# Attention, a gated layer and a normalised layer on one core: the splits move from GpSimd to ScalarE and VectorE, and TensorE gets more filler matmuls around the first scores

## The chip, the core and the metric

One core of a Trainium2 chip runs the whole program. The metric is the device time of one execution in microseconds (us); "before" is the median of three runs. The profile is of one more execution of the same program, recorded by the hardware profiler. Its engines are TensorE (PE, with PEld for its weight loads), VectorE (DVE), ScalarE (ACT), GpSimd (POOL) and SyncE (SP, which issues the DMAs).

## The reference, cut to what matters

```python
scores = scale * np.matmul(q, k.transpose(0, 1, 3, 2))     # q, k, v: 2 x 12 heads x 448 x 64
scores = np.where(mask, -1e9, scores)                       # causal
attn = softmax(scores); attn_out = np.matmul(attn, v)
x = attn_out as (896 tokens, 768)
gate = 1.0 / (1.0 + np.exp(-(x @ w_gate)))                  # w_gate, w_val: 768 x 1536
val = x @ w_val
x = gate * val @ w_out                                      # w_out: 1536 x 768
h = x @ w_in                                                # 768 x 1024
solu = h * softmax(h)
ln = (solu - mean) / np.sqrt(var + 1e-06) * g_ln
out = ln @ w_out2                                           # 1024 x 768
```

## The kernel before, in words

Every product that has to be close to float32 is made of three matmuls in a reduced format (fp32r): a value is split into a **high part** (a copy that rounds) and a **low part** (the value minus the high part), and high x high, high x low and low x high are summed in PSUM. So each tensor that TensorE reads costs two elementwise instructions on some other engine, and the change is about which engine makes them.

**Attention.** Two heads make a pair; there are 12 pairs. A loop of numbered slots, four to a head (96 of them, and some to drain), issues the work of all engines by hand: in slot s the scores of s (`sc_mm`, L350, two slots at a time), the row maximum (`sc_max`, DVE L359), the exponential of slot s-2 (`sc_exp`, ACT L365), and, a few slots later, transposes of the probabilities (`tr_mm`, L416, into one of two PSUM buffers), their split (`tr_hi` on ACT L423, `tr_lo` on DVE L231), the transposes of the reciprocal sums (`rs_mm`, tile r, L388) and the product with v (`pv_mm`, L445). Scores go into one of four PSUM buffers, and a buffer comes free when the exponential has read it. The splits of q, k, v are "side steps": the table `SIDE` gives the slot of each within its pair, `ENG` its engine (A ScalarE, D VectorE, P GpSimd). The names that matter: kh0, kh1 are the high parts of k of the pair's first and second head, kl0, kl1 the low parts, qh and ql those of q. A head's q and k arrive in one buffer (tile qkr) of a ring of four; the load of head h+4 is issued on SP when head h has been split. Each engine takes its instructions in the order in which they were issued, so a step that waits holds up all that stands behind it.

Before the loop, TensorE multiplies an identity matrix 30 times into a PSUM tile that nobody reads (tile warm, L315), and the splits of heads 0 and 1 are issued.

**Gated layer** (L600): 24 chunks of weights, two (gate, value) to each of 12 tiles t; a chunk is a stationary block hl[high, low] of 128 x 768. Weights come from DRAM as 64-bit words (tile raw, two buffers) and are turned into float32 by one ScalarE and three VectorE instructions (`bits_steps`, L112 to L120, tile t). `start_chunk(c)` and `mid_chunk(c)` are called at the beginning and in the middle of the matmuls of chunk c; they prepare chunk c+1 and c+2. A "rider" is a tile of the third layer's weights (wi), prepared in the same way at the middle of certain chunks. After the value chunk the gate is applied (`gate_val`): sigmoid on ACT (L183), product on DVE (L186), high part on ACT (L188), low part on POOL (L189).

**Output projection** (L627, 12 more chunks), **third layer** (L657) and **last product** (L718) follow; `w_hi`, the high part of every weight chunk, is on POOL (L131), `w_lo` on DVE (L135).

Of the kernel before, what the change touches and what calls it, by code (L numbers as in the profile page):

```python
# [44 lines left out]
def attn_moe_moe2(ctx: ExitStack, tc: tile.TileContext, qk, v, w_gv, w_out, w_in2, w_out2, g_ln, out):  # L45
# [87 lines left out]
    def w_lo(it, hi, lo, g=None):
        if g is None:
            nc.vector.tensor_tensor(out=lo, in0=t_t.pop(it), in1=f32(hi), op=ALU.subtract)  # L135
        else:
            nc.vector.scalar_tensor_tensor(out=lo, in0=t_t.pop(it), scalar=g, in1=f32(hi),
                                           op0=ALU.mult, op1=ALU.subtract)
# [54 lines left out]
    with ExitStack() as actx:  # L193
# [122 lines left out]
        for h in range(2):
            prep_k_hi(h)
            prep_q_hi(h)
            if h == 0:
                prep_k_lo(h, 'D', False)  # L320
# [465 lines left out]
```

## Time and profile before

| | |
|---|---|
| three runs | 518.37, 518.78, 519.37 us; median 518.78 |
| profiled execution | 518.95 us, span from the first to the last instruction 517.2 us |
| granted TensorE clock, mean | 0.993 of full speed |
| PE / DVE / ACT / POOL busy | 97% / 70% / 39% / 43% of the span |

The span is what the views below cover; 518.95 - 517.2 = 1.75 us of the execution lie around it. Busy shares are means over stages that differ: in attention all engines are nearly full, after it TensorE alone is.

### The profile page before, as it was taken

The page shows a single profiled execution, that of the slowest core. Times are in us where ns is not written, and L with a number is a line of the kernel's source. Part 1 is how long each engine was busy: PE and PEld are TensorE (multiplying, and loading weights), DVE is VectorE, ACT ScalarE, POOL GpSimd, SP SyncE. Part 2 cuts the span into 40 slices and gives each one's busy share as a digit, 9 for nine tenths or more (in the row PEclk, how much of TensorE's full clock was granted, in tenths as well). Part 3 has the DMA queues.
Part 4 walks back from the last instruction along what each step waited for, and adds up shares of the span by engine and source line. Part 5 has one row for each costly group of instructions (what it writes and reads, how often), then busy time and mean ns, then how long its engine had stood idle before and what let it go on. Part 6 is the DMA issues. An engine that isn't in the chain of part 4 may idle for free. (4 is left out here: it accounts for less than half of the span.)

```text
span 517.2 us, 7582 instructions
## 1 busy us (share of the span) xinstructions
PE 502.7 (97%) x2786; PEld 455.7 (88%) x2786; DVE 360.9 (70%) x542; ACT 200.3 (39%) x446; POOL 220.0 (43%) x299
## 2 busy tenths in 40 slices
PE   5999999989999999999999999999999999999997
PEld 5899898878999988888889899999998888899997
DVE  5998999987565887887787775777872888741210
ACT  5888887874223223232313221221122433332211
POOL 4999999972333133333223330111151577820000
PEclk8899999999999999999999999999999999999999
DMA  7955454112323434334434332344431231000101
GB/s 206 289 156 148 113 150 126 43 61 73 130 104 103 160 125 159 106 107 157 163 125 160 122 116 82 128 163 163 128 123 54 69 116 63 0 32 30 62 32 61
DMA packets 15125, 58.30 MB, mean 113 GB/s; under 512 B 2160, under 2 KB 2672, under 8 KB 15088
## 3 DMA queue, kind: packets, MB, share of 16 engines
q1 hardware_dynamic: 15088, 57.81, 34.9%
q8 instruction: 22, 0.36, 0.3%
q14 instruction: 15, 0.12, 0.1%
HBM read 55.05 MB, written 2.75 MB: 112 GB/s over the span
## 5 line engine op out<-in xcount | busy, mean ns | idle before, releaser
L600 PE MATMUL gv<-xy,hl 128*128 128x448 f32 x828 | 170.5, 367 | 3.0 <-DVE hl L135 3.0
L600 PEld LDWEIGHTS gv<-xy,hl 128*128 128x128 f32 x828 | 154.6, 188 | 18.8 <-DVE hl L135 5.8
L627 PE MATMUL pm<-g,hl 128*128 128x448 f32 x432 | 89.4, 368 | 0.0
L627 PEld LDWEIGHTS pm<-g,hl 128*128 128x128 f32 x432 | 81.1, 188 | 8.2
L112 ACT ACTIVATE raw<-raw 128x768 f32<-128x768 f32 (+1 forms) x56 | 47.4, 857 | 55.0 <-DMA raw<-in_wo_dram 26.7
L115 DVE TENSOR_SCALAR t<-raw 128x768 int32<-128x768 int32 (+1 forms) x56 | 40.9, 730 | 34.3 <-ACT raw L112 33.0
L117 DVE SCALAR_TENSOR_TENSOR t<-raw,t 128x768 int32<-128x768 int32 (+1 forms) x56 | 59.4, 1061 | 1.9
L718 PE MATMUL po<-wo,lt 128*128 128x384 f32 x336 | 60.5, 339 | 0.0
L189 POOL TENSOR_TENSOR g<-wk,g 128x448 fp32r<-128x448 f32 x24 | 27.3, 1158 | 77.8 <-ACT g L188 77.8
L657 PE MATMUL h<-wi,xy 128*128 128x512 f32 x252 | 59.2, 395 | 0.0
L718 PEld LDWEIGHTS po<-wo,lt 128*128 128x128 f32 x336 | 58.7, 188 | 0.1
L657 PEld LDWEIGHTS h<-wi,xy 128*128 128x128 f32 x252 | 47.2, 187 | 11.4
L120 DVE SCALAR_TENSOR_TENSOR t<-raw,t 128x768 int32<-128x768 int32 (+1 forms) x56 | 54.9, 980 | 1.7
L131 POOL TENSOR_SCALAR hl<-t 128x768 fp32r<-128x768 f32 x36 | 34.0, 943 | 42.6 <-PE pm L627 31.6
L365 ACT ACTIVATE p<-s,sum 128x448 f32<-128x448 f32 (+1 forms) x96 | 45.5, 480 | 16.0 <-DVE sum L359 16.0
L445 PE MATMUL x<-pt,v 128*128 128x448 f32 (+3 forms) x252 | 48.7, 327 | 0.0
L350 PE MATMUL s<-qks 128*128 128x448 f32 (+1 forms) x192 | 42.8, 321 | 4.0 <-ACT p L365 2.5
L445 PEld LDWEIGHTS x<-pt,v 128*128 128x128 f32 x252 | 37.1, 190 | 2.0 <-ACT rb L221 1.3
L350 PEld LDWEIGHTS s<-qks 128*128 128x128 f32 x192 | 32.4, 199 | 6.9 <-POOL qks L231 3.2
L359 DVE TENSOR_REDUCE sum<-s 128x1 f32<-128x448 f32 (+1 forms) x96 | 36.3, 409 | 0.9 <-PE s L350 0.9
L135 DVE TENSOR_TENSOR hl<-t,hl 128x768 fp32r<-128x768 f32 x36 | 34.3, 952 | 3.7 <-POOL hl L131 3.6
L131 POOL TENSOR_SCALAR wi<-t 128x512 fp32r<-128x512 f32 x12 | 7.4, 618 | 66.3 <-DVE t L120 66.3
(90 smaller groups left out, 583.6 us busy)
## 6 DMA issues: line engine op xcount, KB each, us to landing
raw<-in_gv_dram SPq DMA_DIRECT2D x24, 768.0 KB, 4.3
raw<-in_wo_dram SPq DMA_DIRECT2D x20, 768.0 KB, 4.3
qkr<-in_qk_dram SPq DMA_DIRECT2D x46, 224.0 KB, 4.0
raw<-in_wi_dram SPq DMA_DIRECT2D x12, 512.0 KB, 3.5
vr<-in_v_dram SPq DMA_DIRECT2D x12, 256.0 KB, 2.8
out_dram<-o SPq DMA_DIRECT2D x6, 384.0 KB, 2.3
qkr<-in_qk_dram SPq DMA_DIRECT2D x4, 112.0 KB, 2.6
out_dram<-o SPq DMA_DIRECT2D x2, 192.0 KB, 1.9
```

The costliest lines, as they stand in the source:

```text
L112: nc.scalar.activation(out=w1.bitcast(F32), in_=w1.bitcast(F32), func=AF.Copy, scale=2.0 ** -112)
L115: nc.vector.tensor_scalar(out=tt, in0=w1, scalar1=3, scalar2=None, op0=ALU.logical_shift_left)
L117: nc.vector.scalar_tensor_tensor(out=tt, in0=w1, scalar=-2 ** 31, in1=tt, op0=ALU.bitwise_and, op1=ALU.bitwise_or)
L120: nc.vector.scalar_tensor_tensor(out=tt, in0=w0, scalar=29, in1=tt, op0=ALU.logical_shift_right, op1=ALU.bitwise_or)
L131: nc.gpsimd.tensor_scalar(out=hi, in0=t_t[it], scalar1=g, scalar2=1.0, op0=ALU.mult, op1=ALU.mult)
L350: nc.tensor.matmul(out=o, lhsT=l, rhs=r, start=(m == 0), stop=(m == 2))
L365: nc.scalar.activation(out=p_t[h % NPB][:, POFF[i]:POFF[i] + n], in_=ps_sc.pop(s), func=AF.Exp, bias=mx, scale=1.0, accum_out=sm)
L445: nc.tensor.matmul(out=ps[:, 128 * j:], lhsT=l, rhs=pt_t[h][:, c, u, c0:c0 + S - 128 * j], start=(n == 0), stop=(n == 20))
L600: nc.tensor.matmul(out=ps[i, b], lhsT=w[:, a, cs], rhs=xy[kk][:, x, b * S:(b + 1) * S], start=(kk == 0 and a == 0 and x == 0), stop=(kk == ...
L627: nc.tensor.matmul(out=ps[b], lhsT=w[:, a, cs], rhs=g_t[kk][:, x, b * S:(b + 1) * S], start=(kk == 0 and a == 0 and x == 0), stop=(kk == N ...
L657: nc.tensor.matmul(out=h[:, n * 512:(n + 1) * 512], lhsT=xy[kk][:, a, tk], rhs=wi[n * NK + kk][:, c], start=(kk == 0 and i == 0), stop=(kk ...
L718: nc.tensor.matmul(out=ps[n], lhsT=lts[k // 4][:, a, k % 4], rhs=wo[k][:, c, cs], start=(k == 0 and i == 0), stop=(k == NF2 - 1 and i == 2))
```

## The change

1. `w_hi` (the high parts of the chunks and the riders) goes from GpSimd to ScalarE. In the last stage the two uses of it keep GpSimd.
2. The gate's low part goes from GpSimd to VectorE, and is issued one step later, behind the products of both batches.
3. `chunk_lo(c + 1)` moves from the middle of chunk c to its start, ahead of the bit steps of chunk c+2; riders move from chunks 6, 8, ..., 20 to 7, 9, ..., 21.
4. In attention kh0 goes from VectorE to ScalarE, kl0 from GpSimd to VectorE, and ql0, ql1, kl0 change slots.
5. Around the start: 56 filler matmuls in place of 30, and 24, 8 and 8 more behind the scores of slots 2, 4 and 6; q's high part of head 0 on VectorE; the low parts of head 1 are issued inside the loop, behind the maxima of slots 0 and 1; small moves among the memsets.

```diff
-    rider = {6 + 2 * n: n for n in range(8)}
+    rider = {7 + 2 * n: n for n in range(8)}
...
-    def w_hi(it, hi, g=1.0):
-        nc.gpsimd.tensor_scalar(out=hi, in0=t_t[it], scalar1=g, scalar2=1.0, op0=ALU.mult, op1=ALU.mult)
...
+    def w_hi(it, hi):
+        nc.scalar.copy(out=hi, in_=t_t[it])
...
     def start_chunk(c):
         chunk_hi(c + 1)
+        chunk_lo(c + 1)
...
     def mid_chunk(c):
-        chunk_lo(c + 1)
...
         nc.scalar.copy(out=g[:, 0], in_=gf)
-        nc.gpsimd.tensor_tensor(out=g[:, 1], in0=gf, in1=f32(g[:, 0]), op=ALU.subtract)
+        yield
+        nc.vector.tensor_tensor(out=g[:, 1], in0=gf, in1=f32(g[:, 0]), op=ALU.subtract)
         yield
...
-        ENG = dict(rx='P', qh0='P', qh1='P', kh0='D', kh1='A', kl0='P', kl1='P', vh='P', vl='P', xh='A', xl='P', rr='A', lk='P')
+        ENG = dict(rx='P', qh0='P', qh1='P', kh0='A', kh1='A', kl0='D', kl1='P', vh='P', vl='P', xh='A', xl='P', rr='A', lk='P')
...
-        for _ in range(30):
-            nc.tensor.matmul(out=ps[:, :128], lhsT=identb, rhs=identb, start=True, stop=True)
...
+        keep_warm(56)
+        prep_k_hi(0)
+        prep_k_lo(0, 'D', False)
+        prep_q_hi(0, 'D')
+        prep_q_lo(0)
+        prep_k_hi(1)
+        prep_q_hi(1)
+        load_qk(4)
...
         SIDE = dict(
-            rm=12, rx=10, ql1=-2, rc=10, xh=22, qh0=-7, kh0=-6, xm=21, ql0=-4, sm=9, kl0=-1, qh1=-4, kh1=-3, kl1=-1,
+            rm=12, rx=10, ql1=-1, rc=10, xh=22, qh0=-7, kh0=-6, xm=21, ql0=-5, sm=9, kl0=-3, qh1=-4, kh1=-3, kl1=-1,
...
             at(sc_mm, s)
+            if s in (2, 4, 6):
+                keep_warm(24 if s == 2 else 8)
...
             at(sc_max, s)
+            if s == 0:
+                prep_k_lo(1, 'D', False)
+            if s == 1:
+                prep_q_lo(1)
+                load_qk(5)
...
                         ev[b].send(ps[1, b])
+                for b in bs:
+                    if i:
+                        next(ev[b])
...
-            w_hi(("o", k), wo[k][:, 0])
+            nc.gpsimd.tensor_scalar(out=wo[k][:, 0], in0=t, scalar1=1.0, scalar2=1.0, op0=ALU.mult, op1=ALU.mult)
```

**VectorE before the first scores and just after.** The line numbers of the two versions differ by a few: L231 and L228 are the low parts of k (64x448) and of the transposes (pt), L252 and L249 the low part of q, L359 and L355 a row maximum (tile sum). Before:

```order
L231 TENSOR_TENSOR qks<-qkr,qks 64x448
L252 SCALAR_TENSOR_TENSOR qks<-qkr,qks 128x448 x2
L359 TENSOR_REDUCE sum_148<-s 128x1 x2
L225 CAST qks<-qkr 128x448
L359 TENSOR_REDUCE sum_148<-s 128x1 x2
```

and in the change:

```order
L228 TENSOR_TENSOR qks<-qkr,qks 64x448
L242 TENSOR_SCALAR qks<-qkr 128x448
L249 SCALAR_TENSOR_TENSOR qks<-qkr,qks 128x448
L355 TENSOR_REDUCE sum_148<-s 128x1
L228 TENSOR_TENSOR qks<-qkr,qks 64x448
L355 TENSOR_REDUCE sum_148<-s 128x1
L249 SCALAR_TENSOR_TENSOR qks<-qkr,qks 128x448
L355 TENSOR_REDUCE sum_148<-s 128x1
```

The first maximum no longer stands behind q's low part of head 1 (the second of the "x2"), and k's low part of head 1 (the second 64x448) is now VectorE's.

**VectorE over the second half of a pair in attention.** L225 is kh0, L452 and L448 scale a finished pair by the reciprocal sums (xf). Before:

```order
L225 CAST qks<-qkr 128x448
L231 TENSOR_TENSOR pt<-t,pt 128x512
L359 TENSOR_REDUCE sum_150<-s 128x1 x2
L252 SCALAR_TENSOR_TENSOR qks<-qkr,qks 128x448
L231 TENSOR_TENSOR pt<-t,pt 128x512
L359 TENSOR_REDUCE sum_150<-s 128x1
L452 TENSOR_TENSOR xf<-x,rb 128x448
L359 TENSOR_REDUCE sum_150<-s 128x1
L252 SCALAR_TENSOR_TENSOR qks<-qkr,qks 128x448
L231 TENSOR_TENSOR pt<-t,pt 128x512
L359 TENSOR_REDUCE sum_150<-s 128x1 x2
```

and in the change:

```order
L228 TENSOR_TENSOR pt<-t,pt 128x512
L355 TENSOR_REDUCE sum_150<-s 128x1
L249 SCALAR_TENSOR_TENSOR qks<-qkr,qks 128x448
L355 TENSOR_REDUCE sum_150<-s 128x1
L228 TENSOR_TENSOR pt<-t,pt 128x512
L355 TENSOR_REDUCE sum_150<-s 128x1
L448 TENSOR_TENSOR xf<-x,rb 128x448
L228 TENSOR_TENSOR qks<-qkr,qks 64x448
L355 TENSOR_REDUCE sum_150<-s 128x1
L228 TENSOR_TENSOR pt<-t,pt 128x512
L355 TENSOR_REDUCE sum_150<-s 128x1
L249 SCALAR_TENSOR_TENSOR qks<-qkr,qks 128x448
```

The cast kh0 is gone, kl0 (64x448) has come in, and each q low part, which stood right ahead of a transposes' low part (pt), now stands between two maxima.

**VectorE in the gated layer, from one value chunk to the next.** L115, L117 and L120 are the three bit steps (768 wide a chunk, 512 wide a rider), L135 and L134 the low parts of a chunk (hl) or a rider (wi), L186 and L182 the gate's product (wk). Before:

```order
L135 TENSOR_TENSOR wi_2519<-t,wi_2519 128x512
L115 TENSOR_SCALAR t<-raw 128x768
L117 SCALAR_TENSOR_TENSOR t<-raw,t 128x768
L120 SCALAR_TENSOR_TENSOR t<-raw,t 128x768
L135 TENSOR_TENSOR hl<-t,hl 128x768
L186 TENSOR_TENSOR wk<-gv,wk 128x448 x2
L115 TENSOR_SCALAR t<-raw 128x768
```

and in the change, where L186 is the gate's low part (g):

```order
L134 TENSOR_TENSOR hl<-t,hl 128x768
L115 TENSOR_SCALAR t<-raw 128x768
L117 SCALAR_TENSOR_TENSOR t<-raw,t 128x768
L120 SCALAR_TENSOR_TENSOR t<-raw,t 128x768
L115 TENSOR_SCALAR t<-raw 128x512
L117 SCALAR_TENSOR_TENSOR t<-raw,t 128x512
L120 SCALAR_TENSOR_TENSOR t<-raw,t 128x512
L182 TENSOR_TENSOR wk<-gv,wk 128x448 x2
L186 TENSOR_TENSOR g_2483<-wk,g_2483 128x448 x2
L134 TENSOR_TENSOR hl<-t,hl 128x768
L134 TENSOR_TENSOR wi_2518<-t,wi_2518 128x512
```

The low part of the next chunk has moved from behind the chunk's three bit steps to ahead of them, and the gate's two low parts have come in behind its products.

**ScalarE over the same stretch.** L112 is its part of the bit steps, L183 and L179 the sigmoid, L188 and L184 the gate's high part. Before:

```order
L112 ACTIVATE raw<-raw 128x768
L112 ACTIVATE raw<-raw 128x512
L183 ACTIVATE wk<-gv 128x448 x2
L112 ACTIVATE raw<-raw 128x768
L188 CAST g_2427<-wk 128x448 x2
```

and in the change, where L131 is `w_hi`:

```order
L131 CAST hl<-t 128x768
L112 ACTIVATE raw<-raw 128x768
L179 ACTIVATE wk<-gv 128x448 x2
L131 CAST hl<-t 128x768
L112 ACTIVATE raw<-raw 128x768
L112 ACTIVATE raw<-raw 128x512
L131 CAST wi_2518<-t 128x512
L184 CAST g_2483<-wk 128x448 x2
```

Each chunk's high part now stands ahead of ScalarE's share of the bit steps, and the rider's high part stands ahead of the gate's.

## Rows read from the trace of the kernel before

**Rows 1.** The page: busy time of each engine; the chain that ended last.

```profile
PE 502.7 (97%) x2786; PEld 455.7 (88%) x2786; DVE 360.9 (70%) x542; ACT 200.3 (39%) x446; POOL 220.0 (43%) x299
...
PE 44%; ACT 0%; issue 0%
```

**Rows 2.** Waits: engine, line, waited for; us in total, times, longest us.

```profile
PEld gv L600 <- DVE hl L135: 5.8, 8, 0.9
...
PEld r L388 <- POOL rx L223: 2.9, 9, 1.2
...
PEld t L416 <- PE s L350: 1.7, 8, 0.2
```

**Rows 3.** Windows around the first scores: busy us (instructions) of each engine, granted clock.

```profile
7.90:10.40 2.50, 0.03 (x1) 0.00 (x0) 2.00 (x5) 1.21 (x5) 2.33 (x3) 0.68 1.03 227
10.40:15.70 5.30, 5.16 (x23) 4.42 (x24) 3.67 (x9) 4.25 (x16) 3.99 (x6) 0.50 1.05 270
```

**Rows 4.** Timeline of the start: start us, duration us, instruction, [idle before].

```profile
1.61 3.38 PE L315 MATMUL warm<-identb 128*128 128x128 bf16 x30 [1.61 <-DVE identb L289]
...
4.74 0.62 DVE L231 TENSOR_TENSOR qks<-qkr,qks 64x448 fp32r<-64x448 f32 x1 [1.07 <-ACT qks L221]
...
6.69 0.82 PE L350 MATMUL s<-qks 128*128 128x448 f32 x4
...
7.71 0.56 ACT L221 CAST qks<-qkr 128x448 fp32r<-128x448 f32 x1 [3.00 <-DMA qkr<-in_qk_dram]
...
8.37 0.63 DVE L252 SCALAR_TENSOR_TENSOR qks<-qkr,qks 128x448 fp32r<-128x448 f32 x1 [1.74 <-POOL qks L242]
...
8.91 0.75 DVE L359 TENSOR_REDUCE sum<-s 128x1 f32<-128x448 f32 x2
...
9.69 0.55 DVE L225 CAST qks<-qkr 128x448 fp32r<-128x448 f32 x1
...
10.44 0.77 PE L350 MATMUL s<-qks 128*128 128x448 f32 x2 [2.51 <-ACT p L365]
```

**Rows 5.** Timeline of TensorE: the first transpose of r in three pairs.

```profile
26.61 0.30 PE L388 MATMUL r<-identx,rx 128*128 128x128 f32 x1
...
35.09 0.33 PE L388 MATMUL r<-identx,rx 128*128 128x128 f32 x1
...
97.32 0.33 PE L388 MATMUL r<-identx,rx 128*128 128x128 f32 x1
```

**Rows 6.** Window over seven pairs of attention, columns as in rows 3.

```profile
35.09:97.32 62.23, 61.79 (x478) 55.93 (x477) 57.48 (x120) 50.64 (x161) 59.99 (x85) 1.00 0.46 119
```

**Rows 7.** Groups in that window, by form: xcount | busy us, mean ns | idle before.

```profile
L231 POOL TENSOR_TENSOR qks<-qkr,qks 64x448 fp32r<-64x448 f32 x14 | 18.5, 1341 | 0.0
...
L252 DVE SCALAR_TENSOR_TENSOR qks<-qkr,qks 128x448 fp32r<-128x448 f32 x14 | 14.4, 1029 | 0.0
...
L225 DVE CAST qks<-qkr 128x448 fp32r<-128x448 f32 x7 | 4.8, 680 | 0.0
```

**Rows 8.** Windows after attention: tile t=2; t=6; t=4 to 11; second output tile.

```profile
149.00:163.58 14.58, 14.58 (x73) 13.52 (x72) 9.17 (x10) 3.67 (x6) 4.20 (x4) 1.00 0.30 103
208.22:223.48 15.26, 14.86 (x74) 13.39 (x72) 12.17 (x15) 4.47 (x7) 4.81 (x5) 1.00 0.42 139
...
178.18:300.47 122.29, 119.27 (x577) 107.23 (x576) 95.43 (x110) 34.89 (x55) 37.89 (x39) 1.00 0.41 139
...
315.35:330.23 14.88, 14.88 (x73) 13.52 (x72) 11.06 (x14) 3.36 (x5) 2.25 (x3) 1.00 0.31 109
```

**Rows 9.** Timeline at the start of tile t=6.

```profile
208.59 0.95 DVE L135 TENSOR_TENSOR hl<-t,hl 128x768 fp32r<-128x768 f32 x1
...
209.59 1.48 PE L600 MATMUL gv<-xy,hl 128*128 128x448 f32 x6 [0.40 <-DVE hl L135]
```

**Rows 10.** Groups from 194.33 to 300.47 us, by form, columns as in rows 7.

```profile
L189 POOL TENSOR_TENSOR g<-wk,g 128x448 fp32r<-128x448 f32 x14 | 15.9, 1159 | 40.6 <-ACT g L188 40.6
...
L112 ACT ACTIVATE raw<-raw 128x768 f32<-128x768 f32 x14 | 12.7, 905 | 20.0 <-DMA raw<-in_gv_dram 20.0
```

More of the change, by code (lines that the diff above doesn't have):

```diff
@@ L128, in bits, with w_lo @@
             pass
-    def w_hi(it, hi, g=1.0):
-        nc.gpsimd.tensor_scalar(out=hi, in0=t_t[it], scalar1=g, scalar2=1.0, op0=ALU.mult, op1=ALU.mult)
[L133 to L138, printed above, removed]
+    def w_hi(it, hi):
+        nc.scalar.copy(out=hi, in_=t_t[it])
+    def w_lo(it, hi, lo):
+        nc.vector.tensor_tensor(out=lo, in0=t_t.pop(it), in1=f32(hi), op=ALU.subtract)
     def chunk_hi(c):
@@ L244, in prep_q_hi @@
             else:
-                nc.scalar.activation(out=t[:, 1], in_=qk_raw[h][:, 0], func=AF.Copy, scale=0.125)
+                nc.vector.tensor_scalar(out=t[:, 1], in0=qk_raw[h][:, 0], scalar1=0.125, scalar2=None, op0=ALU.mult)
         def prep_k_hi(h, eng='A'):
@@ L253, in prep_q_lo, with prep_k_lo @@
                                            op0=ALU.mult, op1=ALU.subtract)
-        def prep_k_lo(h, eng='P', last=True):
+        def prep_k_lo(h, eng='P', load=True):
             t = qk_sp[h]
             sub(eng, t[D:, 0], qk_raw[h][D:, 1], f32(t[D:, 0]))
-            if last:
-                qk_raw.pop(h)
+            if load:
                 load_qk(h + 4)
@@ L285, in attn_moe_moe2 @@
         make_identity(nc, ident)
-        nc.gpsimd.tensor_copy(out=identx[:, :D], in_=ident[:, D:])
-        nc.gpsimd.tensor_copy(out=identx[:, D:], in_=ident[:, :D])
         nc.vector.tensor_copy(out=identb, in_=ident)
@@ L291, in attn_moe_moe2 @@
         nc.gpsimd.memset(mask0, 0.0)
+        nc.gpsimd.tensor_copy(out=identx[:, :D], in_=ident[:, D:])
+        nc.gpsimd.tensor_copy(out=identx[:, D:], in_=ident[:, :D])
         nc.gpsimd.affine_select(out=mask0, in_=mask0, pattern=[[-1, 128]], compare_op=ALU.is_ge,
@@ L307, in attn_moe_moe2 @@
                 nc.vector.memset(p_t[i][:, POFF[j] + QE[j]:POFF[j + 1]], 0.0)
-            nc.vector.memset(p_t[i][:, POFF[3] + QE[3]:], 0.0)
         for i in range(2):
@@ L311, in attn_moe_moe2, with keep_warm @@
                 nc.scalar.copy(out=v2[i][:, a, :, D:2 * D], in_=zero.rearrange("p (j d) -> p j d", j=3))
+            nc.vector.memset(p_t[i][:, POFF[3] + QE[3]:], 0.0)
         ps = ps_x.tile([128, S], F32, tag="x", name="warm")
-        for _ in range(30):
-            nc.tensor.matmul(out=ps[:, :128], lhsT=identb, rhs=identb, start=True, stop=True)
[L316 to L320, printed above, removed]
-                prep_q_lo(h)
-            else:
-                prep_q_lo(h)
-                prep_k_lo(h, 'P', False)
-            qk_raw.pop(h)
-            load_qk(h + 4)
+        def keep_warm(n):
+            for _ in range(n):
+                nc.tensor.matmul(out=ps[:, :128], lhsT=identb, rhs=identb, start=True, stop=True)
+        keep_warm(56)
[6 more added lines that the diff above has]
+        load_qk(4)
         rs_t, rx_t, rb_t, pt_t, ps_sc, ps_tr, ps_pv, ps_rr, xf_t = {}, {}, {}, {}, {}, {}, {}, {}, {}
@@ L565, in attn_moe_moe2 @@
             ev.send(pre[t, 1])
+            next(ev)
     gpb = gctx.enter_context(tc.tile_pool(name="gpb", bufs=1, reuse_waits="tile"))
```

## The prediction, made before the changed kernel ran

> **What bounds the kernel now.** I read the page first: TensorE is busy 97% of the span, the next engine 70%, and the chain that ended last is TensorE alone [rows 1]. So only time in which TensorE stands still, or runs at half its clock, can be won, and the other engines matter only where they make it wait. Then the list of waits [rows 2] and windows by stage. Three places come out.
>
> *The start.* TensorE idles from 7.9 to 10.4 us, the granted clock falls to 0.50 meanwhile (1.2 GHz in place of 2.4; the mean of that stretch is 0.68), and the next 5.3 us of matmuls run at 0.50 [rows 3].
>
> *Attention.* The first transposes of r are a pair's mark: 26.61 to 35.09 is 8.48 us, 35.09 to 97.32 is 7 pairs of 8.89 [rows 5]. TensorE's work is the same in each, so every later pair loses about 0.41 us. The waits name two places, each once per pair: r waits for rx, GpSimd's last step in a row of them, and a transposes' group t waits some 0.2 us [rows 2]. The "PE s" named there cannot be it, as TensorE always runs behind its own scores; what the group needs is one of two PSUM buffers, freed by VectorE's tr_lo. GpSimd is busy 59.99 of 62.23 us, VectorE 57.48, ScalarE 50.64 [rows 6].
>
> *The gated layer.* A tile's 72 matmuls take 14.58 us undisturbed (t=2) and 15.26 in t=6 [rows 8]. The fifth matmul of t=6, the first that reads a low part, starts at 209.59, when VectorE's hl has ended (208.59 + 0.95) [rows 9]; eight such waits are listed [rows 2]. From t=4 to 11 the stage takes 122.29 us where 8 x 14.58 = 116.64 would do: 5.65 us lost.
>
> **The change, part by part.**
>
> *Gated layer.* The late hl stands behind three bit steps of another chunk, and these wait for a load: ScalarE's share of them stood idle 20.0 us for the DMA in 14 chunks [rows 10]. With the low part ahead of the bit steps, it needs only its high part, whose chunk landed one chunk earlier. I walk one tile from TensorE's first matmul, 0. VectorE makes two products (0.62 each, 209.46 on, just behind that hl), ScalarE two high parts of the gate behind them (0.56 each, as the cast at 7.71 [rows 4]), to about 2.1. The chunk's high part on ScalarE is not in the trace; nearest is its 768-wide L112, 905 ns [rows 10] (bounds 0.56, a 448-wide cast, and 0.96, that scaled to 768): to 3.0. Low part 0.95 [rows 9]: ready at 4.0, wanted at 7.3 (half a tile). Slack 3.3 us. The value chunk: sigmoids to 8.6, high part 9.5, low part 10.4, wanted at 14.6: slack 4.2. The gate's low part on VectorE is new: GpSimd takes 1159 ns [rows 10]; the nearest VectorE rows of two SBUF operands and 448 columns are 0.62 us when GpSimd is quiet (at 4.74 and 8.37 [rows 4]) and 1029 when not [rows 7]. GpSimd has nothing left to do here, so 0.62; 1.24 a tile. VectorE's work becomes 12.17 + 1.24 = 13.4 of 14.58 [rows 8], less what GpSimd's absence shortens. It fits. What is queued behind the new waits: ScalarE's high part of the rider waits for VectorE's bit steps at about 14.8, and the gate's high parts stand behind it; they are not wanted before VectorE's products at 15 anyway. Of the 5.65 us I take back 4.9: the listed waits, 5.8 [rows 2], include in each the little that lies between any two loads, and the rest of the loss is a slightly wider spacing of some matmuls (below), which I leave. Bounds 0 and -5.7.
>
> *Attention.* kl0 takes 1341 ns on GpSimd [rows 7], a share of 15% of a pair; without it rx can come up to 1.3 us earlier, and r no longer waits. On VectorE it costs 0.62 (at 4.74 [rows 4]); kh0 goes, 0.68 [rows 7], and costs ScalarE 0.56 (at 7.71 [rows 4]). VectorE's sum hardly changes: 57.48 + 7 x (0.62 - 0.68) = 57.1 over seven pairs, which at 8.48 have 59.4 us: 96%. But the order does: a q low part of 1029 ns stood right ahead of tr_lo; now a maximum, or 0.62 of kl0, does. 1029 is the price beside GpSimd's 1341; alone it is 0.63 (at 8.37 [rows 4]), so VectorE falls below 96%. ScalarE: 50.64 + 7 x 0.56 = 54.6, 92%. I take 0.36 of 0.41 us in seven pairs, -2.5. Bounds: 0, and -2.9.
>
> *Start.* The first maximum no longer waits for head 1 (8.91 before, [rows 4]; about 7.6 now, when the scores that begin at 6.69 are done). k's low part of head 1 on VectorE follows its high part (7.71 + 0.56) and is ready at 8.9. But slot 5 needs the PSUM buffer of slot 1, and ScalarE's exponential of slot 1 now stands behind kh of head 2, whose load lands near 9.6 (the cast at 9.69 [rows 4]). So the scores of slot 4 and 5 start near 10.5 again, not earlier. The gain is the clock: 5.16 us of matmuls at 0.50 [rows 3] take about half at full clock, 2.6 less. The fillers: 30 took 3.38 us [rows 4], 0.107 from start to start when the last one's length is taken off, and 128 columns at 1.2 GHz are 0.107 us: the low level. At 6.69 the level was the high one, four score matmuls in 0.82 us against two in 0.77 at 10.44 [rows 4]. So the clock rose between 4.9 and 6.7. If in the middle, near 5.5, some 36 of the 56 are done by then and 20 more at half the price end at 6.6: the scores start on time. If late, 56 x 0.107 end at 7.6 and the scores are 0.9 late. The 24 lie in what was idle. The two groups of 8 are paid: 16 x 0.055 = 0.9. Waits for exponentials, and scores that start a little late, take some 0.4 back. I take -1.3; bounds -2.6, when the fillers hide in waits, and +1.7, when the clock falls all the same and the 16 cost 0.107.
>
> What the row shows is one execution with 0.50 from about 9 to 15.7 us [rows 3], and one place of the rise. The Trainium skill ("TensorE: Matmul & The Clock Gate", section "What's actually happening") says that the gate does not start its count with the kernel, so that the place where the clock rises shifts from run to run. By the row the sum below stands at 510.2; by the page the start can come out at the worse bound in some runs, which is the second rival's time. No single trace can show which.
>
> *Edits at nothing.* The memsets lie in the wait for the first load. The rider's shift by one chunk moves work off VectorE's even chunk. Loads of head 4 and 5 follow the same splits as before; the order of chunk loads changes by one place. In the output projection TensorE did not wait (14.88, x72, busy all through [rows 8]); ScalarE has 3.36 of 14.88 there and takes on 2 x 0.9.
>
> **Sum.** 518.95 (the profiled execution: span 517.2 and 1.75 around it) - 4.9 - 2.5 - 1.3 = 510.25; the median of the runs is 0.17 lower. Predicted: 510.2.
>
> **Rivals.**
>
> 1. *Attention keeps 8.89 us a pair*, because ScalarE takes the wait over: kh0 now stands between two exponentials, and one of them frees the PSUM buffer of the next scores. For: ScalarE goes to 92%. Against: it has 59.4 - 54.6 = 4.8 us left in seven pairs, 0.7 in each, and takes on 0.56 once a pair, not ahead of every score. Time: 510.2 + 2.5 = 512.7.
> 2. *The clock falls at the start as before*, since TensorE still idles some 0.5 to 1 us between the fillers and the scores of slot 4, or since the 56 begin at a bad moment. The second is what the skill's page would have. For: 2.5 us of idling were enough before [rows 3]. Against: less than half of that is left. The start then gives +0.5 in place of -1.3: 512.0.
> 3. *ScalarE in the gated layer*: chunk high parts, waiting behind the gate's, come too late, and half of the stalls return. For: ScalarE takes its instructions in order, and the gate's wait for TensorE. Against: over 3 us of slack. 510.2 + 2.45 = 512.7.
> 4. *VectorE becomes the bound of the gated layer; slower than before.* In t=6 it works 12.17 of 15.26 us and waits 3.1 [rows 8]. If all its waits stay, 1.24 more makes a tile 16.5: 8 tiles x (16.5 - 14.58) = 15.4 in place of 5.65, +9.7 - 2.5 - 1.3 on 518.95: 524.7 after the 0.17. It decides where waits exceed 14.58 - 13.41 = 1.2 us a tile. Against: GpSimd, whose work beside VectorE's stretched it (0.63 against 1.03 [rows 4, 7]), is out of this stage, so the 12.17 shrinks.
>
> One thing more shifts the sum without being a rival: 72 matmuls take 14.58 us in the gated layer but 14.88 in the output projection [rows 8], same shape, no wait. If a stage takes on the other's spacing, that is 6 x 0.30 = 1.8 less or 11 x 0.30 = 3.3 more.
>
> **How the numbers follow.** Forecast 0.60; rival 1 0.15; rival 2 0.08; rival 3 0.07; rival 4 0.05; nothing moves, or gains cancel, 0.05. What a measurement can tell from no change is about 0.2%, 1 us. Forecast and rivals 1 to 3 are faster: 0.90, less 0.02 for two of them together with the wider spacing: 0.88 faster, 0.06 same, 0.06 slower. The range: below, the spacing's 1.8 and the attention's and start's other bounds, 507.0; above, rivals 1 to 3 and two of them at once, 515.0.
>
> **What will show it.** Right: pairs of 8.5 us between r's; no wait of TensorE for hl and tiles of 14.6; granted clock 1.00 from about 5 us on; GpSimd idle in the gated layer. Wrong: a wait of the scores for ScalarE's p (rival 1), 0.50 between 9 and 16 us (2), hl waiting for ScalarE (3), VectorE over 95% in a tile of over 15 us (4). What would make me wrong most is a wait whose place in the order I walked with a duration taken from a quieter stretch.

## The result, and the profile after

The changed kernel takes 513.98 us (median of 4 runs, 513.41 to 514.42) against 518.58 (4 runs, 517.47 to 519.37) of the kernel before: a ratio of 0.9912, 95% interval 0.9891 to 0.9933. It is 4.6 us faster where 8.4 were forecast; the time lies in the range given. Most kernels here, the one before too, have some executions 2 to 5 us longer than the rest, with a wider spacing of the matmuls (last section), so I compare stages of profiled executions and say where their spacing differs. The profiled execution took 514.42 us, 2.45 of it outside the span.

The page of the changed kernel; the busy times, then the chain that ended last by line:

```profile
PE 501.6 (98%) x2852; PEld 459.5 (90%) x2852; DVE 350.8 (69%) x567; ACT 239.5 (47%) x505; POOL 136.2 (27%) x214
...
PE gv L604 33%; PE pm L634 17%; PE po L725 12%; PE h L664 11%; DVE sum L355 3%; DVE qks L249 3%; DVE pt L228 2%; PE s L346 2%; PE t L412 1%; DVE xf L448 1%; PE x L441 1%; DVE qks L228 1%; PE tp L707 1%; PE r L384 1%; ACT p L361 1%
```

Three lines of VectorE stand in the chain, sum (L355), qks (L249) and pt (L228): in attention the end now goes through VectorE. The waits that answer to [rows 2]:

```profile
PEld s L346 <- ACT p L361: 9.1, 22, 0.9
...
PEld r L384 <- POOL rx L220: 1.9, 2, 1.1
...
PE s L346 <- ACT p L361: 1.6, 4, 0.6
```

The wait of gv for hl is gone, that of a transposes' group t too, and that of r for rx comes twice, not nine times. In their place the scores wait for ScalarE's exponentials, 22 times. Windows that answer to [rows 3, 6, 8]: the start, seven pairs of attention, the tile t=6:

```profile
7.90:10.40 2.50, 2.00 (x29) 1.67 (x27) 2.28 (x6) 1.83 (x7) 1.00 (x2) 1.00 1.02 234
10.40:15.70 5.30, 4.87 (x47) 4.26 (x48) 5.13 (x11) 4.63 (x16) 2.17 (x3) 1.00 1.07 275
...
35.87:99.40 63.53, 62.18 (x478) 56.48 (x477) 59.57 (x120) 54.19 (x169) 51.98 (x78) 1.00 0.44 117
...
208.41:223.00 14.59, 14.59 (x74) 13.52 (x73) 11.33 (x17) 6.48 (x10) 0.00 (x0) 1.00 0.43 144
```

The granted clock is 1.00 all through the start. Seven pairs take 63.53 us, 9.08 each, where they took 62.23. A gated tile takes 14.59, and GpSimd does nothing in it. By stage, from first instruction to first instruction:

| stage | before | after | difference | forecast |
|---|---|---|---|---|
| up to the first transpose of r | 18.55 | 18.65 | +0.10 | -1.3 |
| from there to the twelfth pair's | 96.25 | 98.15 | +1.90 | -2.5 |
| from there to the gated layer | 12.30 | 12.26 | -0.04 | 0 |
| gated layer | 173.37 | 167.81 | -5.56 | -4.9 |
| output projection | 89.28 | 87.55 | -1.73 | 0 |

With +0.13 behind these the span is 5.20 us shorter; 0.67 came back outside it. So the gated layer gave what was forecast, the projection took the narrower spacing that was named as open, and attention went the wrong way. No run shows that the edits chose that spacing; without its 1.73 us the profiled spans differ by 3.5.

Where the 9.08 come from, in the timeline of one pair:

```profile
57.95 1.14 POOL L228 TENSOR_TENSOR xy<-xf,xy 128x448 fp32r<-128x448 f32 x1
...
58.16 1.42 DVE L249 SCALAR_TENSOR_TENSOR qks<-qkr,qks 128x448 fp32r<-128x448 f32 x1
...
59.50 0.34 DVE L355 TENSOR_REDUCE sum<-s 128x1 f32<-128x192 f32 x1
...
59.94 0.42 ACT L361 ACTIVATE p<-s,sum 128x192 f32<-128x192 f32 x1 [0.98 <-DVE sum L355]
...
60.50 0.19 PEld L346 LDWEIGHTS s<-qks 128*128 128x128 f32 x1 [0.38 <-ACT p L361]
...
61.63 0.56 ACT L218 CAST qks<-qkr 128x448 fp32r<-128x448 f32 x1
...
62.02 0.67 DVE L249 SCALAR_TENSOR_TENSOR qks<-qkr,qks 128x448 fp32r<-128x448 f32 x1
...
62.08 0.32 ACT L361 ACTIVATE p<-s,sum 128x64 f32<-128x64 f32 x1
...
62.19 1.38 POOL L228 TENSOR_TENSOR v<-vr,v 128x384 fp32r<-128x384 f32 x1
...
62.54 0.19 PEld L346 LDWEIGHTS s<-qks 128*128 128x128 f32 x1 [0.35 <-ACT p L361]
```

Two waits a pair. (a) ql1, one slot later now, runs at 58.16 for 1.42 us; the maximum behind it starts at 59.50, the exponential at 59.94 after 0.98 us of idling, and TensorE's scores stand 0.38 us for the PSUM buffer which that exponential frees. ql1 is long as well as late: a GpSimd difference began 0.21 us ahead of it, at 57.95, while ql0, which begins at 62.02 ahead of GpSimd's 62.19, takes 0.67. (b) kh0, the CAST at 61.63, holds ScalarE for 0.56 us; the exponential behind it starts at 62.08, and the scores stand 0.35 us.

### The profile page after: what moved, and what is told of

The parts are those of the page before. It is cut to its first block, busy times and chain, and to the rows that moved or that the text cites. A ratio compares the mean times of both kernels' runs of the same rounds, so it can differ in the third digit from the quotient of the medians.

```text
span 512.0 us, 7710 instructions
## 1 busy us (share of the span) xinstructions
PE 501.6 (98%) x2852; PEld 459.5 (90%) x2852; DVE 350.8 (69%) x567; ACT 239.5 (47%) x505; POOL 136.2 (27%) x214
## 4 chain that ended last, share of the span: by engine, by line
PE 81%; DVE 12%; ACT 2%; issue 2%; POOL 1%; DMA 1%; SPq 1%; DVEq 0%; POOLq 0%; ACTq 0%
PE gv L604 33%; PE pm L634 17%; PE po L725 12%; PE h L664 11%; DVE sum L355 3%; DVE qks L249 3%; DVE pt L228 2%; PE s L346 2%; PE t L412 1%; DVE xf L448 1%; PE x L441 1%; DVE qks L228 1%; PE tp L707 1%; PE r L384 1%; ACT p L361 1%
## 5 line engine op out<-in xcount | busy, mean ns | idle before, releaser
L604 PE MATMUL gv<-xy,hl 128*128 128x448 f32 x828 | 168.0, 365 | 0.0
L634 PE MATMUL pm<-g,hl 128*128 128x448 f32 x432 | 87.7, 365 | 0.0
L651 POOL TENSOR_SCALAR t<-t,g_sb 128x768 f32<-128x768 f32 x8 | 9.0, 1128 | 248.7 <-PE pm L634 248.7
L134 DVE TENSOR_TENSOR hl<-t,hl 128x768 fp32r<-128x768 f32 x36 | 34.5, 958 | 41.0 <-ACT hl L131 39.3
L117 DVE SCALAR_TENSOR_TENSOR t<-raw,t 128x768 int32<-128x768 int32 (+1 forms) x56 | 53.4, 954 | 1.9
L112 ACT ACTIVATE raw<-raw 128x768 f32<-128x768 f32 (+1 forms) x56 | 47.9, 865 | 10.5 <-DMA raw<-in_wo_dram 6.1
L120 DVE SCALAR_TENSOR_TENSOR t<-raw,t 128x768 int32<-128x768 int32 (+1 forms) x56 | 51.2, 913 | 1.7
L346 PE MATMUL s<-qks 128*128 128x448 f32 (+1 forms) x192 | 46.4, 321 | 3.3 <-ACT p L361 1.6
L355 DVE TENSOR_REDUCE sum<-s 128x1 f32<-128x448 f32 (+1 forms) x96 | 38.6, 413 | 1.6 <-PE s L346 1.1
L171 DVE TENSOR_TENSOR lt<-tp,lt 128x512 fp32r<-128x512 f32 x14 | 9.7, 691 | 36.4 <-ACT lt L170 36.4
L115 DVE TENSOR_SCALAR t<-raw 128x768 int32<-128x768 int32 (+1 forms) x56 | 31.1, 555 | 4.4 <-ACT raw L112 4.4
L131 ACT CAST hl<-t 128x768 fp32r<-128x768 f32 x36 | 30.0, 833 | 7.3 <-PE pm L634 4.2
```

What stands on the lines that cost most here:

```text
L112: nc.scalar.activation(out=w1.bitcast(F32), in_=w1.bitcast(F32), func=AF.Copy, scale=2.0 ** -112)
L117: nc.vector.scalar_tensor_tensor(out=tt, in0=w1, scalar=-2 ** 31, in1=tt, op0=ALU.bitwise_and, op1=ALU.bitwise_or)
L120: nc.vector.scalar_tensor_tensor(out=tt, in0=w0, scalar=29, in1=tt, op0=ALU.logical_shift_right, op1=ALU.bitwise_or)
L346: nc.tensor.matmul(out=o, lhsT=l, rhs=r, start=(m == 0), stop=(m == 2))
L355: nc.vector.reduce_max(out=sums_of(s)[1], in_=ps_sc[s], axis=AX.X, negate=True)
L604: nc.tensor.matmul(out=ps[i, b], lhsT=w[:, a, cs], rhs=xy[kk][:, x, b * S:(b + 1) * S], start=(kk == 0 and a == 0 and x == 0), stop=(kk == ...
```

## The experiments

My theory after this trace: the gated layer holds all the gain; attention loses by waits (a) and (b), each made by one instruction's place; the start's gain is handed to waits for ScalarE and GpSimd. The rivals stand in each expectation. "Pair" is the distance between the first transposes of r of two pairs, as a mean of the seven from the third to the tenth where nothing else is said. Each ratio is to the kernel before as timed beside it (median 518.93 us in experiments 1 to 4, 518.04 in 5 to 8, 517.47 in 9 to 12), so ratios, and stages of traces, are what to compare. Edits are cut to the parts of lines that change.

**1. The gated layer's edits alone.** The kernel before with the diff's first part (rider, w_hi, chunk_lo, gate_val); ENG, SIDE and the start as before.

> The kernel before with the gated layer's edits alone (high parts on ScalarE, gate's low part on VectorE, the chunk's low part moved forward, riders shifted). Theory: all that was won comes from here, 5.6 us in the gated layer and 1.7 in the output projection, and the rest of the change costs some 2: tiles of 14.59 us in both stages, r transposes of attention still 8.89 us apart, 511.3 us. Rival: the two stages need the changed attention's order too (its chunks 0 and 1 are prepared there); then waits for hl stay at some tiles, and the time is 513 to 516.

512.63 us, ratio 0.9906 (0.9872 to 0.9940); pairs 8.89; tiles and output tiles 14.59. There is no wait for hl, and the gated layer takes 167.81 us as in the changed kernel. So these edits alone give the whole gain, with the narrow spacing in the projection; attention keeps its old length. The rival is out; the median is 1.3 us above the theory's.

**2. kh0 back on VectorE.**

```
-kh0='A', kh1='A', kl0='D'
+kh0='D', kh1='A', kl0='D'
```

> The changed kernel with kh0 back on VectorE. Theory (two new waits in each pair, each from one moved step): the wait of the scores of slot 5 for the exponential behind kh0, about 0.23 us, goes; the wait of slot 3's scores behind ql1 stays; pairs of about 8.85 us, 514.0 - 10 x 0.23 = 511.7 us. Rival (the pair is bound by what VectorE has to do in all): VectorE gets 0.68 us more a pair, pairs of 9.3 us or more, 516 us or more.

521.29 us, ratio 1.0089 (1.0052 to 1.0125): slower than before; pairs 9.76. My expectation was wrong, the rival right. The window and the group in attention, one kl0 with the GpSimd step beside it in the timeline, and last the same two steps in the changed kernel:

```profile
36.00:97.00 61.00, 55.28 (x433) 51.08 (x432) 60.44 (x112) 47.79 (x146) 46.67 (x71) 1.00 0.47 124
...
L228 DVE TENSOR_TENSOR qks<-qkr,qks 64x448 fp32r<-64x448 f32 x6 | 9.4, 1570 | 0.2
...
60.15 1.57 DVE L228 TENSOR_TENSOR qks<-qkr,qks 64x448 fp32r<-64x448 f32 x1
...
60.09 1.15 POOL L228 TENSOR_TENSOR qks<-qkr,qks 64x448 fp32r<-64x448 f32 x1 [0.72 <-ACT qks L218]
...
56.24 0.62 DVE L228 TENSOR_TENSOR qks<-qkr,qks 64x448 fp32r<-64x448 f32 x1
...
56.66 1.22 POOL L228 TENSOR_TENSOR qks<-qkr,qks 64x448 fp32r<-64x448 f32 x1 [0.88 <-ACT qks L218]
```

VectorE is busy 60.44 of 61.00 us. kl0 takes it 1570 ns here, where the changed kernel's takes 623: here a GpSimd difference begins just ahead of it, at 60.09, and kl0's 1.57 is about that one's 1.15 and 0.5 more. The Trainium skill ("SBUF — State Buffer", section "SBUF: two separate sides") says that a VectorE operation with two SBUF inputs and a GpSimd operation that reads SBUF take turns at a shared port pair: the one that starts first blocks the other whole. The trace agrees on who waits: 0.62 us where kl0 begins ahead of GpSimd's step (56.24, 56.66), 1.57 where it begins behind (60.15, 60.09). By that rule I estimate 1.09 of waiting and 0.62 of work, 1.71.

**3. ql1 back at its slot.**

```
-rm=12, rx=10, ql1=-1,
+rm=12, rx=10, ql1=-2,
```

> The changed kernel with q's low part of the second head issued one slot earlier again (ql1 -2 in place of -1). Theory (two new waits): the wait of slot 3's scores, about 0.28 us, goes, and the old wait of a transposes' group for VectorE's low part, about 0.2 us, comes back; the wait behind kh0 stays: pairs of 8.95 to 9.05 us, 513 us. Rival (VectorE's sum binds): nothing changes, 9.08 us, 514.0.

512.43 us, ratio 0.9893 (0.9871 to 0.9915); pairs 8.92, a little under the range expected, and not the rival's 9.08. Wait (a) is gone, and the old wait of the transposes for tr_lo is back:

```profile
PEld t L412 <- PE s L346: 3.8, 7, 0.6
```

**4. The table of before** (ENG's kh0 on VectorE and kl0 on GpSimd; ql1=-2, ql0=-4, kl0=-1) with the changed start and gated layer.

> The changed kernel with engines and slots of the side steps of attention as before (kh0 VectorE, kl0 GpSimd, ql0, ql1, kl0 in their old slots); fillers, start and gated layer as changed. Theory: pairs of 8.89 us again, 10 x 0.19 = 2 us less than the changed kernel, 512.0; the start gives nothing either way, so r's first transpose stays near 18.6 us. Rival: if the changed start had won its 1.3 us and the table lost it, r's first transpose comes at 17.3 and the time is 510.7.

513.10 us (12 runs), ratio 0.9920 (0.9891 to 0.9950); pairs 8.91, first r at 18.84, the third at 35.99. Experiment 1, with the same table and the old start, has its third r at 35.18 and a median 0.5 us lower: the changed start gives nothing here. The rival's early r did not come; the median is 1.1 us above the theory's. (The profiled execution, 517.95, has the wide spacing.)

**5. Without the new idle matmuls.**

```
-        keep_warm(56)
+        keep_warm(30)
-            if s in (2, 4, 6):
-                keep_warm(24 if s == 2 else 8)
```

> The changed kernel with 30 idle matmuls ahead of the first scores in place of 56 and without the 24, 8 and 8 among the first slots; all else as changed. Theory A (the clock's lead is handed to waits for ScalarE's exponentials and GpSimd's rx, which do not depend on TensorE's clock): the granted clock falls to 0.50 somewhere between 8 and 16 us again, yet the first transposes of r start at 18.4 to 19.2 us, against 18.65 with the fillers, and the median is within 0.6 us of 513.98. Theory B (the fillers are worth the 1.3 us that I put in the sum, and something else at the start ate it): r starts at 19.9 or later and the median is 515.2 or more.

514.38 us (10 runs), ratio 0.9935 (0.9907 to 0.9962); first r at 18.21, the third at 35.24 against 35.87. Two windows of its start:

```profile
8.00:11.00 3.00, 0.74 (x5) 0.48 (x5) 2.43 (x6) 2.02 (x8) 0.83 (x2) 1.00 1.02 228
11.50:14.50 3.00, 3.00 (x15) 2.52 (x15) 2.89 (x5) 2.33 (x8) 2.16 (x3) 0.50 1.08 289
```

The clock falls to 0.50 (1.2 GHz) after that idling, TensorE is busy all of the second window at half speed, and r still comes earlier than with the fillers, 0.2 us earlier than theory A has it. In the changed kernel they buy nothing.

**6. kh0 one slot later on ScalarE**, behind the exponential of slot 1, not ahead of it.

```
-qh0=-7, kh0=-6,
+qh0=-7, kh0=-5,
```

> The changed kernel with kh0 one slot later on ScalarE, behind the exponential of slot 1 and the next transposes' split, in place of ahead of that exponential. Theory A (two waits a pair of about 0.25 us each: one made by kh0 ahead of an exponential, one by ql1 ahead of a maximum): the second wait goes, pairs fall from 9.08 to 8.80 to 8.90 us, the median to about 512.0. Theory B (the pair is set by VectorE's sum of work, 57.2 us in seven pairs plus what it waits, and the place of kh0 on ScalarE does not matter): pairs stay at 9.0 to 9.1, the median at 514.

511.01 us (4 runs), ratio 0.9880 (0.9823 to 0.9937); pairs 8.75, somewhat shorter than theory A's. Half of the waits for the exponential go:

```profile
PEld s L346 <- ACT p L361: 2.7, 7, 0.4
```

In the same stretch (36 to 97 us) the changed kernel has 13 of them. VectorE does the same work in both, so rival B is out. One number in a table, 0.33 us a pair in the trace; the intervals of the two ratios overlap.

**7. Both, kh0 later and ql1 back.**

> The changed kernel with kh0 one slot later on ScalarE and ql1 back at its old place. Theory A: both waits go, pairs are 8.60 to 8.80 us, the median 510.5 to 511.5. Theory B (VectorE's sum binds): pairs as with ql1 alone put back, 8.9 to 8.95, the median 512.4; the wait shows again at a transposes' group for VectorE's tr_lo.

513.81 us (7 runs, three of them with the wide spacing, 516.99 to 517.68), ratio 0.9930 (0.9894 to 0.9966); pairs 8.88. The two edits don't add: with ql1 back the transposes wait for tr_lo as in experiment 3 (3.9 us, 7 times), whatever kh0 does. The rival's numbers were right; its reason, VectorE's sum, isn't shown by this, as ql1's place makes the wait in both.

**8. kh0 alone on ScalarE**, one slot later; kl0 on GpSimd and all other places as before.

```
-kh0='A', kh1='A', kl0='D'        ql1=-1, kh0=-6, ql0=-5, kl0=-3
+kh0='A', kh1='A', kl0='P'        ql1=-2, kh0=-5, ql0=-4, kl0=-1
```

> The changed kernel with the table's places of before (ql1, ql0, kl0), kl0 back on GpSimd, and kh0 alone moved from VectorE to ScalarE, one slot later than changed. VectorE then does 0.68 us a pair less than before and nothing more. Theory A (VectorE's place in the order and its sum set one wait, GpSimd's row of steps ahead of rx the other): the wait of the transposes for tr_lo goes, that of r for rx stays, pairs 8.65 to 8.80 us, median 510.5 to 512. Theory B (GpSimd, at 60.0 of 62.2 us before, binds the pair as long as kl0 is on it): pairs stay at 8.85 to 8.90, median 512.5 to 513.

511.30 us (4 runs), ratio 0.9861 (0.9835 to 0.9886). Pairs of two lengths, an early one (the second has 8.35 too) and a late one:

```profile
36.33:44.68 8.35, 8.35 (x71) 8.00 (x69) 7.16 (x16) 7.69 (x25) 8.03 (x13) 1.00 0.54 142
53.51:62.42 8.91, 8.66 (x70) 8.05 (x69) 7.08 (x17) 7.72 (x26) 8.59 (x13) 1.00 0.56 136
...
PEld s L346 <- POOL qks L228: 2.0, 5, 0.4
```

At 8.35 TensorE is busy all the time: that is a pair's floor. From the fourth pair on the scores wait for GpSimd's kl0: GpSimd has 8.59 us a pair of work, more than 8.35. It idles for more than 0.15 us nowhere between 28 and 97 us, and its kl0 returns after 8.86 us already in the early pairs (29.52, 38.38), so it falls behind until it sets the pace at 8.90. Between 35 and 97 us the kernel before has no such idling of GpSimd either: its 8.89 was GpSimd's. Theory A holds for VectorE and in the median, B for GpSimd.

**9. kl0 on VectorE in every other pair**, the rest as in experiment 8.

```
+            STEP[f"kl{a}"] = (lambda p, a=a: prep_k_lo(2 * p + a, ENG[f"kl{a}"]) if a or p % 2 else None), ENG[f"kl{a}"]
+        STEP["kl0d"] = (lambda p: None if p % 2 else prep_k_lo(2 * p, "D")), "D"     # SIDE: kl0d=-3
```

> The kernel of the experiment before (kh0 on ScalarE one slot later, the other places as before), with kl0 on VectorE in every other pair and on GpSimd in the rest. There the first pairs took 8.35 us, GpSimd busy 8.03 of them, and only from the fourth on did GpSimd's sum of 8.6 us a pair stretch them to 8.90. Theory A (a pair is set by whichever of VectorE and GpSimd has the larger sum, stretched by the other's work): with GpSimd at 8.6 less half of 1.34, about 7.9 us a pair, and VectorE at 7.1 plus half of 0.8 to 1.3, no engine binds and pairs stay at 8.35 to 8.55 all through; the median is 3 us under the 511.3 of that kernel, 507.5 to 509.5. Theory B (an order that alternates makes a wait of its own, or the two engines stretch each other): pairs of 8.7 or more on average, no gain over 511.3.

510.32 us (4 runs, one of them 515.11), ratio 0.9874 (0.9814 to 0.9933); profiled 510.08, the shortest of all. Two pairs in a row, and the wait in the longer ones:

```profile
35.13:44.02 8.89, 8.51 (x70) 8.01 (x69) 8.53 (x18) 7.69 (x25) 7.68 (x12) 1.00 0.48 135
44.02:52.36 8.34, 8.34 (x70) 8.00 (x69) 7.66 (x17) 7.68 (x25) 8.02 (x13) 1.00 0.51 141
...
PEld t L412 <- PE s L346: 2.6, 4, 0.8
```

GpSimd keeps up (7.7 to 8.0), and the pairs without kl0 on VectorE are at the floor. Those with it wait for tr_lo again, 8.9. VectorE has 8.53 us of work there, more than the floor: kl0, and q low parts of 1.21 and 1.44 us behind GpSimd differences where the next pair's take 1.05 and 0.61. Whether its sum or its order makes the wait was not separated. The mean of the eight pairs from the second r on is 8.66. Theory A's range was missed by 0.8 us. By the ratios (0.9861 there, 0.9874 here) no gain over experiment 8 is shown, so B's "no gain" stands.

**10. The same without the new idle matmuls** (edit as in 5).

> The same with the alternating kl0, and with 30 idle matmuls ahead of the first scores, none later. Theory A (the idle matmuls buy nothing, since the start waits for ScalarE's and GpSimd's steps): r's third pair starts 0.3 to 0.7 us earlier than with them, as it did when they were taken from the changed kernel, and the median is level to 0.7 us lower. Theory B (with faster pairs the clock at the start matters, since no later wait absorbs it): 0.5 to 1.3 us higher.

511.42 us (4 runs), ratio 0.9886 (0.9837 to 0.9935), 1.1 over experiment 9, as theory B has it, with intervals that overlap. TensorE's scores between 5 and 17 us (ns: shortest, median, longest), here and in experiment 9:

```profile
L346 PE MATMUL s<-qks x21: 255/615/740, 6.0 to 16.7; 128*128 128x448 f32 x6, 128*128 128x64 f32 x6, 128*128 128x320 f32 x5, 128*128 128x192 f32 x4
```

```profile
L346 PE MATMUL s<-qks x24: 192/371/469, 6.4 to 16.2; 128*128 128x448 f32 x6, 128*128 128x64 f32 x6, 128*128 128x320 f32 x6, 128*128 128x192 f32 x6
```

By these durations nearly all of the start ran at the low level in this execution (a median of 615 ns against 371; the trace's mean granted clock, 1.000, does not show it), and the third r comes at 35.80 against 35.13. With the same 30 idle matmuls and the same first scores, experiment 5's granted clock was 1.00 up to 11 us. So the level at the start differs by execution, as the Trainium skill has it ("TensorE: Matmul & The Clock Gate", section "What's actually happening": the gate does not begin with the kernel). The fillers' worth lies between nothing (5) and about 1 us (here).

**11. The chunk's low part behind the bit steps again.**

```
-        chunk_lo(c + 1)          # in start_chunk
+        chunk_lo(c + 1)          # in mid_chunk
```

> The changed kernel with the next chunk's low part put back to the middle of a chunk, behind the bit steps, as before; all else in the gated layer as changed (high parts on ScalarE, the gate's low part on VectorE). Theory A (the low part's place behind bit steps that wait for a load was the cause of the stalls): waits of gv's weight loads for VectorE's hl come back and the gated layer takes 170 to 173.5 us in place of 167.8 where both have the spacing of 14.59 a tile. Theory B (VectorE's operations, stretched by GpSimd's work beside them, were the cause, and GpSimd's absence the cure): it stays at 167.8 to 168.5 without such waits.

513.28 us (4 runs), ratio 0.9906 (0.9879 to 0.9934); the gated layer 167.81 us, tiles 14.59, no wait of TensorE for hl. The cause named in the prediction, theory A, was wrong; B's result came.

**12. The gate's low part back on GpSimd.**

```
-        nc.vector.tensor_tensor(out=g[:, 1], in0=gf, in1=f32(g[:, 0]), op=ALU.subtract)
+        nc.gpsimd.tensor_tensor(out=g[:, 1], in0=gf, in1=f32(g[:, 0]), op=ALU.subtract)
```

> The changed kernel with the gate's low part back on GpSimd; all else as changed. Theory A (order is what cured the stalls, the engine of the gate's low part is without effect): no wait for hl, tiles at 14.59 (or 14.88, the spacing of the output projection, all through), though VectorE's bit steps go from 954 to about 1060 ns while GpSimd works. Theory B (GpSimd's work beside VectorE's is what made hl late): hl waits return in the tiles with riders, 2 us or more over the stage.

514.47 us (10 runs), ratio 0.9944 (0.9917 to 0.9971); the gated layer 167.81 us, no wait of TensorE for hl. Here theory A's times were right; the bit steps that it saw stretched were not (0.55 and 0.96 us). Neither edit is needed by itself; what they have in common is shown below.

## Why the prediction was right or wrong

**The total.** 513.98 lies in the range, in the part kept for two rivals at once, with a little over half of the forecast gain. That owes something to luck: of the three terms one came out in size for a cause that was wrong, one with the wrong sign, one at nothing, and 1.73 of the 5.20 us between the spans are a spacing that the prediction named but left out of its sum.

**Gated layer: the sum right (-4.9; -5.56 measured), the cause wrong.** The prediction said that "the late hl stands behind three bit steps of another chunk, and these wait for a load", and that the low part's new place cures it. Experiment 11 puts it back behind them, and nothing is lost. The trace of before, read once more around t=6, has a closed loop in it (VectorE, ScalarE, then the loads' issues with their median time to landing):

```profile
199.71 0.96 DVE L120 SCALAR_TENSOR_TENSOR t<-raw,t 128x768 int32<-128x768 int32 x1
...
206.12 0.56 DVE L115 TENSOR_SCALAR t<-raw 128x768 int32<-128x768 int32 x1 [0.57 <-ACT raw L112]
206.72 0.96 DVE L117 SCALAR_TENSOR_TENSOR t<-raw,t 128x768 int32<-128x768 int32 x1
...
212.05 1.40 DVE L115 TENSOR_SCALAR t<-raw 128x768 int32<-128x768 int32 x1 [1.45 <-ACT raw L112]
213.49 1.47 DVE L117 SCALAR_TENSOR_TENSOR t<-raw,t 128x768 int32<-128x768 int32 x1
214.99 0.96 DVE L120 SCALAR_TENSOR_TENSOR t<-raw,t 128x768 int32<-128x768 int32 x1
...
205.18 0.91 ACT L112 ACTIVATE raw<-raw 128x768 f32<-128x768 f32 x1 [3.28 <-DMA raw<-in_gv_dram]
210.11 1.10 ACT L188 CAST g<-wk 128x448 fp32r<-128x448 f32 x2 [4.02 <-DVE wk L186]
211.11 1.67 ACT L112 ACTIVATE raw<-raw 128x768 f32<-128x768 f32 x2
...
raw<-in_gv_dram SPq DMA_DIRECT2D x4, 768.0 KB, 4.4
```

A chunk's last bit step ends at 200.67 and lets the next load go; 4.4 us later ScalarE scales it (205.18), VectorE does bits, hl and the products (206.12 to 210.6), ScalarE the gate's high parts (210.11) and the next scaling (211.11), VectorE the bits (212.05), and the last of these starts at 214.99: 15.28 us after 199.71, the tile's 15.26. The load is in the loop, and so are two bit steps that take 1.40 and 1.47 us beside GpSimd's work where the same two took 0.56 and 0.96 a half tile earlier: 1.35 us, twice the 0.68 by which the loop exceeds 14.58. Without them it would take an estimated 13.9, less than the tile's matmuls. In experiment 11 the step after the scaling is 0.56 again, and in 12 too:

```profile
213.32 0.56 DVE L115 TENSOR_SCALAR t<-raw 128x768 int32<-128x768 int32 x1 [0.32 <-ACT raw L112]
```

```profile
214.88 0.55 DVE L115 TENSOR_SCALAR t<-raw 128x768 int32<-128x768 int32 x1
...
211.26 2.29 POOL L186 TENSOR_TENSOR g<-wk,g 128x448 fp32r<-128x448 f32 x2 [12.31 <-ACT g L184]
```

In 12 GpSimd's two operations lie beside a low part that has time, not beside bits. What is shown: the stalls need neither the low part's old place nor the gate's low part on GpSimd alone. What is argued: the stretched bits in the loop were enough to make them. What stays open: the rider's shift and the high parts on ScalarE were not tried alone, so the share of each is unknown; I had put the shift among the "edits at nothing".

**Attention: the sign wrong (-2.5; +1.9 measured).** The step that failed is "1029 is the price beside GpSimd's 1341; alone it is 0.63 (at 8.37 [rows 4]), so VectorE falls below 96%". The row at 8.37 is not one without GpSimd. Its step began just behind and was the one stretched:

```profile
8.42 1.56 POOL L231 TENSOR_TENSOR qks<-qkr,qks 64x448 fp32r<-64x448 f32 x1
```

The mean of the q low parts stayed where it was beside the GpSimd steps that remain:

```profile
L249 DVE SCALAR_TENSOR_TENSOR qks<-qkr,qks 128x448 fp32r<-128x448 f32 x14 | 14.7, 1047 | 0.0
...
L228 DVE TENSOR_TENSOR qks<-qkr,qks 64x448 fp32r<-64x448 f32 x7 | 4.4, 623 | 0.2
```

This mean hides two prices: ql1 takes 1.42 or 1.43 us in each of the seven pairs and ql0 0.67 (1.05 and 1.00 before), as the one begins behind a GpSimd difference and the other ahead of one. VectorE was busy 59.57 us in seven pairs, not 57.1 or less. kl0 itself cost the 0.62 that I took, and the old waits went as the prediction said. But I moved the 1029 from ahead of tr_lo without asking what it stands ahead of next: a maximum, whose exponential frees the scores' PSUM buffer. That is wait (a), which experiment 3 takes away. Wait (b) is rival 1's mechanism, right down to the instruction; I had priced it at no gain, and it is a loss of 0.33 us a pair (experiment 6). The pair of 8.53 that I forecast lies above the floor of 8.35 (experiment 8), but no run held it: the best mean is 8.66.

**Start: -1.3 forecast, +0.1 measured.** The clock held, as forecast, so rival 2 did not come about. The step that failed is "5.16 us of matmuls at 0.50 [rows 3] take about half at full clock, 2.6 less": they do, but the start is not made of them. Slots 8 and 9 start 1.1 us earlier than before, and then TensorE waits:

```profile
10.53 0.30 PE L346 MATMUL s<-qks 128*128 128x64 f32 x1 [0.64 <-ACT p L361]
...
15.31 0.35 PE L346 MATMUL s<-qks 128*128 128x192 f32 x1 [0.30 <-ACT p L361]
```

The lead is gone at the first r, which waits for rx. By these waits ScalarE and GpSimd set the start's length. Experiments 4 and 5 show no gain from it, experiment 10 at most 1 us from the fillers.

**Rivals 3 and 4** did not come: tiles of 14.59, VectorE busy 11.33 of them where I had worked out 13.4; without GpSimd beside it, its operations shrank as I said.

**The open term.** The output projection's 1.73 us came by the spacing alone, 6 x 0.29.

**Slips in the working**, none of which changes the outcome: 510.25 less the 0.17 is 510.1; the terms given for the range's lower end make 506.7; the start's worse bound is +1.7 in one place, and +0.5, as rival 2's price, in another.

## What to carry to other kernels

When a long instruction is moved out of the way of one wait, walk on to the next instruction behind its new place and to the buffer which that one frees; in a table of slots the place of one short copy was worth 0.33 us a pair. Take the price of a VectorE step from a row in which it begins on the same side of its GpSimd neighbour: ql1 and ql0 are the same instruction at 1.42 and 0.67 us. Balance the sums of the engines that are beside each other as well as their order: pairs stayed at the floor of 8.35 us only until GpSimd, with more work than that, had fallen behind (experiment 8). Before a stall is put down to the instruction named as its releaser, close the loop behind it, loads included, and see what in it is longer than it has to be.

## What the runs showed of the hardware

*Two spacings of the same matmuls.* The gated layer's and the projection's matmuls (448 columns, granted clock 1.00, no waits) run 72 in 14.59 us or 72 in 14.88, 202.6 or 206.7 ns each, and in the changed kernels' traces one of the two holds through both stages. The page of the changed kernel, and that of experiment 6:

```profile
L604 PE MATMUL gv<-xy,hl 128*128 128x448 f32 x828 | 168.0, 365 | 0.0
```

```profile
L604 PE MATMUL gv<-xy,hl 128*128 128x448 f32 x828 | 171.3, 368 | 0.0
```

The 828 + 432 matmuls of the two stages make 5 us of it. In experiment 4 twelve runs of one kernel fall into 512.08 to 513.38 and 516.97 to 518.72, and its profiled one, 517.95, has the wide spacing. The edits don't decide it, as one kernel has both. In the kernel before, the projection has 14.88 and the tile t=2 14.58 in one execution. What chooses between the two is not settled.

*One VectorE operation at two prices.* A 448-wide difference of two SBUF operands took 623 ns or 1570 (experiment 2); a 768-wide shift with one operand took 0.56 or 1.40 us; a q low part 0.67 or 1.42. In each case a GpSimd operation that had begun earlier lay beside the longer one. Where VectorE's began first, GpSimd's was the longer: 1.56 us at 8.42 before, against 1.15 in experiment 2.
